# Fewer, larger zero fills and a mask on the smaller operand in a decode step with cache gradients

## The chip, the cores and the metric

One core of a Trainium2 chip. The metric is the device time of one execution in microseconds (us); a difference below 2% counts as "the same".

## The reference

One token passes through a layer norm, attention over the last 4096 of 32768 cached positions (16 heads on 8 cache heads of 256), and a gated feed-forward block; then the gradients for all inputs are formed. Only this matters here:

```python
W = min(4096, max(256, Sk // 4))                      # 4096 of Sk = 32768
k = jnp.repeat(k_cache[:, :, Sk - W:, :], rep, axis=1)
v = jnp.repeat(v_cache[:, :, Sk - W:, :], rep, axis=1)
...
_out, _vjp = jax.vjp(_f, A_x, A_k_cache, A_v_cache, A_wq, A_wo, B_w_gate, B_w_up, B_w_down)
return (_out0, *_grads)                                # shortened; two of the gradients: 8 x 32768 x 256 bf16 each
```

Seven eighths of the two cache gradients are zeros, and the kernel has to write them: 280.6 MB written against 53.7 MB read.

## The kernel before

GpSimd's queue carries the zero fills, one region of 2 MB (128 partitions x 16 KB) a transfer, from a block of zeros in SBUF. SyncE's queue carries the cache loads, the outputs and a few late fills. Fills 0 to 41 use the whole block of zeros. Then the upper half of the block is lent to weights, and 13 fills go out "in halves" from the lower half. When the weights are used, VectorE clears the upper half again and the other fills follow.

```python
ZW = 8192                       # 16 KB of zeros in each partition
HALF0, HALF1 = 42, 55
...
def send_fills(n0, n1, halves=False):
    for reg in fills[n0:n1]:
        if halves:
            ZQ.dma_start(out=reg.rearrange("p (k f) -> p k f", k=2),
                         in_=zeros[:, 0:ZW // 2].unsqueeze(1).to_broadcast([128, 2, ZW // 2]))
        else:
            ZQ.dma_start(out=reg, in_=zeros)          # ZQ = nc.gpsimd

send_fills(0, HALF0)
send_fills(HALF0, HALF1, True)
...                                                   # first pass over K and V, then the feed-forward blocks
            if n == 1:
                nc.vector.memset(ar(ZW // 2, ZW // 2), 0.0)      # the "clearing"
                send_fills(HALF1, len(fills) - 1)
...                                                   # second pass, per cache head:
            nc.vector.tensor_copy(out=rT[:], in_=r_ps[:])
            ...
            RB_ = Rbig[it % 2]
            nc.vector.tensor_tensor(out=RB_, in0=R_sb[:].unsqueeze(1).to_broadcast([128, 8, 512]),
                                    in1=tl_f[:].unsqueeze(2).to_broadcast([128, 8, 512]), op=ALU.mult)
            ...
                        nc.tensor.matmul(d_ps[:, qi]..., lhsT=rT[32 * q:32 * (q + 1), :],
                                         rhs=RB_[32 * q:32 * (q + 1), l, :], start=True, stop=True)
```

## Time and profile before

| | before |
|---|---|
| time, median of 6 runs | 797.02 us (796.6 to 797.59) |
| bytes moved | 334.77 MB, mean 421 GB/s |
| last computing instruction ends | 730.7 us |
| VectorE busy | 436.6 us |
| issues of GpSimd's queue | 106 |

The prediction below shows the lines and reads them: the 16 DMA engines are busy from end to end, and the last 63 us are transfers alone. In the profile a "packet" of a DMA queue is one row moved (16 KB in the fills and the cache loads) or one semaphore write of 4 bytes that reports a finished transfer.

### The profile page before, as it was taken

Reading aid. Unit: us, or ns where it says so; the run is one execution under the profiler, and the core shown is the slowest. Engines: PE = TensorE matmul, PEld = TensorE weight load, DVE = VectorE, ACT = ScalarE, POOL = GpSimd, SP = SyncE. Lnnn points to the kernel's source line nnn. Section 1 sums busy time; section 2 is a strip of 40 time slices with the busy share of each in tenths; the row PEclk is TensorE's granted clock in tenths of the full one; section 3 lists DMA queues with packets and bytes.
Section 4 is the critical chain, followed back from the end, with each engine's and each line's share of the span. In section 5 each row is a group of like instructions: output and inputs, shape, how many; then the busy total and the mean of one; then the engine's idle time right before and its main releaser. Section 6 shows DMA issues by size and latency. Waiting matters only on the chain.

```text
span 795.1 us, 7301 instructions
## 1 busy us (share of the span) xinstructions
PE 471.2 (59%) x2903; PEld 221.2 (28%) x2926; DVE 436.6 (55%) x629; ACT 196.0 (25%) x309; POOL 63.0 (8%) x115
## 2 busy tenths in 40 slices
PE   0459999999999999251409477673450553722000
PEld 0334434344344433121208334330220210300000
DVE  2116584765846782263690679598653874964000
ACT  0142314134132201010102126362320441534000
POOL 4000000010101111100210001000000000010000
PEclk9989999999999999555558779695555555865555
DMA  9999999999999999999999999999999999999997
GB/s 348 431 427 433 431 427 430 431 429 427 433 420 425 432 416 407 423 420 425 432 432 422 424 430 428 429 424 427 424 427 423 425 424 422 426 421 414 432 432 312
DMA packets 29688, 334.77 MB, mean 421 GB/s; under 512 B 3150, under 2 KB 6230, under 8 KB 8150
## 3 DMA queue, kind: packets, MB, share of 16 engines
q0 software_dynamic: 16832, 216.01, 64.2%
q1 hardware_dynamic: 11382, 116.68, 35.0%
q10 hardware_dynamic: 1440, 1.61, 0.6%
q8 instruction: 23, 0.38, 0.2%
q14 instruction: 11, 0.09, 0.0%
HBM read 53.69 MB, written 280.59 MB: 420 GB/s over the span
## 4 chain that ended last, share of the span: by engine, by line
PE 35%; DMA 34%; DVE 15%; ACT 4%; issue 2%; another core or an unknown queue 0%; SPq 0%; DVEq 0%; ACTq 0%
DMA out_dram<-arena 21%; PE M_ps L317 12%; PE ok_ps L320 7%; PE rows_ps L256 5%; DMA dh_bc<-in_grad_out_dram 4%; DMA arena<-in_A_k_cache_dram 4%; PE tr_ps L253 4%; DMA arena<-in_B_w_down_dram 3%; ACT arena L270 2%; DVE arena L459 2%; PE dqb_ps L502 2%; DMA arena<-in_B_w_gate_dram 2%; DVE arena L635 2%; DVE arena L428 2%; DVE arena L650 1%
## 5 line engine op out<-in xcount | busy, mean ns | idle before, releaser
L312 DVE TENSOR_TENSOR arena<-arena,p_f 128x2048 bf16<-128x2048 bf16 x64 | 145.4, 2286 | 61.3 <-PE M_ps L317 61.2
L317 PE MATMUL M_ps<-arena 128*128 128x512 bf16 x489 | 125.3, 381 | 1.9 <-issue 1.0
L643 PE MATMUL d_ps<-arena,rT 32*128 32x512 bf16 x256 | 46.1, 506 | 115.4 <-DVE arena L651 67.6
L253 PE MATMUL tr_ps<-ident_bf,arena 128*128 128x128 bf16 x1024 | 90.3, 239 | 19.7 <-ACT arena L611 11.4
L256 PE MATMUL rows_ps<-arena,vpad 128*16 128x512 bf16 x256 | 87.4, 436 | 21.0 <-DVE arena L613 15.2
L133 POOL DMA_DIRECT2D out_dram<-arena x89 | 47.4, 535 | 529.9 <-DMA out_dram<-arena 495.9
L253 PEld LDWEIGHTS <-arena 128*128 128x128 bf16 x1024 | 67.6, 107 | 71.4 <-issue 62.2
L270 ACT COPY arena<-tr_ps 128x1024 bf16<-128x1024 bf16 x64 | 61.8, 1016 | 64.5 <-PE tr_ps L253 64.5
L647 ACT CAST arena<-d_ps 128x512 bf16<-128x512 f32 x64 | 37.6, 588 | 125.0 <-PE d_ps L643 124.9
L320 PE MATMUL ok_ps<-arena 128*16 128x512 bf16 x256 | 63.8, 381 | 0.9 <-DVE arena L297 0.9
L317 PEld LDWEIGHTS <-arena 128*128 128x128 bf16 x512 | 43.3, 99 | 59.0 <-issue 23.2
L611 ACT COPY arena<-tr_ps 128x1024 bf16<-128x1024 bf16 x32 | 32.6, 1020 | 95.0 <-PE tr_ps L253 37.1
L651 DVE CAST arena<-d_ps 128x512 bf16<-128x512 f32 x64 | 43.6, 681 | 13.3 <-DMA out_dram<-arena 13.3
L650 DVE CAST arena<-d_ps 128x512 bf16<-128x512 f32 x64 | 43.9, 685 | 12.6 <-PE d_ps L643 12.0
L643 PEld LDWEIGHTS <-rT 32*128 32x128 bf16 x256 | 11.5, 95 | 141.0 <-issue 92.5
L648 ACT CAST arena<-d_ps 128x512 bf16<-128x512 f32 x64 | 38.1, 595 | 14.1 <-DMA out_dram<-arena 14.1
L635 DVE TENSOR_TENSOR arena<-R_sb,tl_f 128x4096 bf16<-128x4096 bf16 x8 | 35.4, 4419 | 0.7 <-ACT R_sb L633 0.7
L256 PEld LDWEIGHTS <-vpad 128*16 128x16 bf16 x256 | 19.0, 91 | 57.6 <-issue 49.5
L320 PEld LDWEIGHTS <-arena 128*16 128x16 bf16 x256 | 19.1, 89 | 41.5 <-issue 20.3
L514 DVE CUSTOM_DVE_ANT_0 arena<-arena 128x4096 bf16<-128x4096 bf16 x3 | 13.1, 4423 | 24.1 <-ACT arena L507 24.1
L285 ACT ACTIVATE e_f<-cols_ps,nbias 128x32 f32<-128x32 f32 x16 | 4.5, 285 | 86.9 <-DVE nbias L281 86.9
L258 DVE COPY arena<-rows_ps 16x512 f32<-16x512 f32 x16 | 10.8, 676 | 26.4 <-PE rows_ps L256 26.3
(199 smaller groups left out, 390.9 us busy)
## 6 DMA issues: line engine op xcount, KB each, us to landing
out_dram<-arena POOLq DMA_DIRECT2D x102, 2048.0 KB, 52.6
out_dram<-arena SPq DMA_DIRECT2D x18, 2048.0 KB, 32.9
arena<-in_A_v_cache_dram SPq DMA_DIRECT2D x10, 2048.0 KB, 50.2
arena<-in_A_k_cache_dram SPq DMA_DIRECT2D x8, 2048.0 KB, 29.3
out_dram<-arena SPq DMA_DIRECT2D x4, 4096.0 KB, 43.8
arena<-in_A_wq_dram SPq DMA_DIRECT2D x2, 3072.0 KB, 20.8
arena<-in_A_wo_dram SPq DMA_DIRECT2D x2, 1792.0 KB, 14.2
out_dram<-arena SPq DMA_DIRECT2D x2, 1792.0 KB, 15.3
```

The costliest lines, as they stand in the source:

```text
L133: ZQ.dma_start(out=reg, in_=zeros)
L253: nc.tensor.transpose(tr_ps[:, dh, i, :], X_sb[:, 4 * q + i, dh * 128:(dh + 1) * 128], ident_bf[:])
L256: nc.tensor.matmul(rows_ps[:], lhsT=pad[:, dh, 16 * q:16 * q + 16], rhs=XT[:, dh].rearrange("p t k -> p (t k)"), start=(q == 0 and dh == 0 ...
L270: sT_ps = dots(kv_at(K_off[g]), KT_slot, vpad[g % 2], rows1, ps_c, "cols", lambda q, XT, ps: nc.scalar.copy(out=XT, in_=ps))
L312: nc.vector.tensor_tensor(out=pK, in0=K_sb[:, 4 * c:4 * c + 4, :].unsqueeze(2).to_broadcast([128, 4, 2, Dh]), in1=p_f[:, c::8, :].unsqueez ...
L317: nc.tensor.matmul(M_ps[:, vh, :], lhsT=V_sb[:, t, vh * 128:(vh + 1) * 128], rhs=pK[:, i, :, :].rearrange("p h d -> p (h d)"), start=(t == ...
L320: nc.tensor.matmul(ok_ps[:].rearrange("p k d -> p (k d)"), lhsT=ppad[g % 2][:, 8 * (t % 4) + t // 4, :], rhs=both(g, t), start=(g == 0 and ...
L635: nc.vector.tensor_tensor(out=RB_, in0=R_sb[:].unsqueeze(1).to_broadcast([128, 8, 512]), in1=tl_f[:].unsqueeze(2).to_broadcast([128, 8, 51 ...
L643: nc.tensor.matmul(d_ps[:, qi].rearrange("p w d -> p (w d)"), lhsT=rT[32 * q:32 * (q + 1), :], rhs=RB_[32 * q:32 * (q + 1), l, :], start=T ...
L648: nc.scalar.copy(out=stK[:, t:t + 2, :], in_=d_ps[:, :, 1, :])
L650: nc.vector.tensor_copy(out=stV[:, t:t + 2, :], in_=d_ps[:, :, 0, :])
L651: nc.vector.tensor_copy(out=stK[:, t:t + 2, :], in_=d_ps[:, :, 1, :])
```

## The change

The intent: fewer and larger transfers on GpSimd's queue, and less VectorE work in the second pass. The mask (which of eight rows l a partition belongs to) is multiplied into the transposed probabilities (128 x 1024) instead of the other operand (128 x 4096); the products are the same.

```diff
+GROUP = 4
     def send_fills(n0, n1, halves=False):
-        for reg in fills[n0:n1]:
+        while n0 < n1:
+            o, g, i = fills[n0]
+            n = 1
+            while n < GROUP and n0 + n < n1 and fills[n0 + n][:2] == (o, g):
+                n += 1
+            reg = zero_rows(o, g, i, i + n, ZW)
             if halves:
                 ... (as before, one transfer a region)
             else:
-                ZQ.dma_start(out=reg, in_=zeros)
+                ZQ.dma_start(out=reg.rearrange("n p f -> p n f"), in_=zeros.unsqueeze(1).to_broadcast([128, n, ZW]))
+            n0 += n
...
-            rT = work2.tile([128, 128], bf16, tag="rT")
-            nc.vector.tensor_copy(out=rT[:], in_=r_ps[:])
+            rTm = rT_slot[it % 2]
+            nc.vector.tensor_tensor(out=rTm, in0=r_ps[:].unsqueeze(1).to_broadcast([128, 8, 128]),
+                                    in1=tl_f[:].unsqueeze(2).to_broadcast([128, 8, 128]), op=ALU.mult)
...
-            RB_ = Rbig[it % 2]
-            nc.vector.tensor_tensor(out=RB_, in0=R_sb..., in1=tl_f..., op=ALU.mult)
-                        nc.tensor.matmul(..., lhsT=rT[32 * q:32 * (q + 1), :], rhs=RB_[32 * q:32 * (q + 1), l, :],
+                        nc.tensor.matmul(..., lhsT=rTm[32 * q:32 * (q + 1), l, :], rhs=R_sb[32 * q:32 * (q + 1), :],
```

More of the change, by code (lines that the diff above doesn't have):

```diff
@@ L87 @@
     rows2 = ar(RB + 47 * KB, 2 * KB)[0:16].bitcast(f32)
-    Rbig = [ar(RB + 8 * KB * i, 8 * KB).rearrange("p (l n) -> p l n", l=8) for i in range(2)]
+    rT_slot = [ar(RB + 2 * KB * i, 2 * KB).rearrange("p (l n) -> p l n", l=8) for i in range(2)]
+    R_slot = [ar(RB + (4 + i) * KB, KB) for i in range(2)]
     dK_off = [RB + 16 * KB, A_off[2]]
@@ L124 @@
                 continue
-            reg = zero_rows(o, g, 0, 5 if g == G - 1 else NZ, ZW)
-            fills += [reg[i] for i in range(reg.shape[0])]
+            fills += [(o, g, i) for i in range(5 if g == G - 1 else NZ)]
     def send_fills(n0, n1, halves=False):
-        for reg in fills[n0:n1]:
+        while n0 < n1:
[4 more added lines that the diff above has]
+            reg = zero_rows(o, g, i, i + n, ZW)
             if halves:
-                ZQ.dma_start(out=reg.rearrange("p (k f) -> p k f", k=2), in_=zeros[:, 0:ZW // 2].unsqueeze(1).to_broadcast([128, 2, ZW // 2]))
-            else:
-                ZQ.dma_start(out=reg, in_=zeros)
+                for r in range(n):
+                    ZQ.dma_start(out=reg[r].rearrange("p (k f) -> p k f", k=2), in_=zeros[:, 0:ZW // 2].unsqueeze(1).to_broadcast([128, 2, ZW // 2]))
+            elif n == 1:
+                ZQ.dma_start(out=reg[0], in_=zeros)
+            else:
+                ZQ.dma_start(out=reg.rearrange("n p f -> p n f"), in_=zeros.unsqueeze(1).to_broadcast([128, n, ZW]))
+            n0 += n
     send_fills(0, HALF0)
@@ L631 @@
                     nc.tensor.matmul(R_ps[:, w, dh, :], lhsT=Zr[:, 2 * w + dh].rearrange("p k i -> p (k i)"), rhs=ident_bf[:], start=True, stop=True)
-            R_sb = work2.tile([128, 512], bf16, tag="R", bufs=1)
-            nc.scalar.copy(out=R_sb[:], in_=R_ps[:].rearrange("p w e n -> p (w e n)"))
-            RB_ = Rbig[it % 2]
-            nc.vector.tensor_tensor(out=RB_, in0=R_sb[:].unsqueeze(1).to_broadcast([128, 8, 512]),
-                                    in1=tl_f[:].unsqueeze(2).to_broadcast([128, 8, 512]), op=ALU.mult)
+            R_sb = R_slot[it % 2]
+            nc.scalar.copy(out=R_sb, in_=R_ps[:].rearrange("p w e n -> p (w e n)"))
             stV, stK = V_sb, kv_at(dK_off[it % 2])
@@ L642 @@
                         q = 2 * qp + qi
-                        nc.tensor.matmul(d_ps[:, qi].rearrange("p w d -> p (w d)"), lhsT=rT[32 * q:32 * (q + 1), :], rhs=RB_[32 * q:32 * (q + 1), l, :],
+                        nc.tensor.matmul(d_ps[:, qi].rearrange("p w d -> p (w d)"), lhsT=rTm[32 * q:32 * (q + 1), l, :], rhs=R_sb[32 * q:32 * (q + 1), :],
                                          start=True, stop=True)
@@ L658 @@
                 nc.vector.memset(ar(ZW, ZW), 0.0)
-        flat = fills[-1].rearrange("p f -> (p f)")
+        o, g, i = fills[-1]
+        flat = zero_rows(o, g, i, i + 1, ZW)[0].rearrange("p f -> (p f)")
         base = 0
```

## The prediction

> **What bounds the kernel now.** I looked first at the page's 40 slices and its DMA queue rows, because the kernel writes two cache gradients that are mostly zeros and so has to move a great many bytes whatever it computes.
>
> ```profile
> DMA  9999999999999999999999999999999999999997
> GB/s 348 431 427 433 431 427 430 431 429 427 433 420 425 432 416 407 423 420 425 432 432 422 424 430 428 429 424 427 424 427 423 425 424 422 426 421 414 432 432 312
> DMA packets 29688, 334.77 MB, mean 421 GB/s; under 512 B 3150, under 2 KB 6230, under 8 KB 8150
> q0 software_dynamic: 16832, 216.01, 64.2%
> q1 hardware_dynamic: 11382, 116.68, 35.0%
> ```
>
> No slice but the last is under nine tenths. q0 is GpSimd's queue (the zero fills), q1 is SyncE's. Their shares of the 16 engines' time, 64.2% and 35.0%, with 0.6% and 0.2% for two small queues, add up to 100% of the span: there is no unused DMA time in the body of this kernel. The second view is the table by stretches, which shows where the little idle time sits (columns: stretch, its length, busy time of the five engine rows, TensorE clock, DMA share, GB/s).
>
> ```profile
> 0.00:20.00 20.00, 0.37 (x1) 0.09 (x1) 4.55 (x18) 1.28 (x1) 9.46 (x18) 1.00 0.92 351
> 20.00:300.00 280.00, 256.95 (x1546) 110.02 (x1570) 163.87 (x163) 75.91 (x112) 21.56 (x39) 0.98 1.01 428
> 700.00:732.00 32.00, 6.25 (x41) 1.38 (x41) 17.55 (x22) 11.32 (x21) 2.39 (x4) 0.51 1.01 418
> 732.00:745.00 13.00, 0.00 (x0) 0.00 (x0) 0.00 (x0) 0.00 (x0) 0.00 (x0) 0.50 1.02 423
> 745.00:760.00 15.00, 0.00 (x0) 0.00 (x0) 0.00 (x0) 0.00 (x0) 0.00 (x0) 0.50 1.00 430
> 780.00:785.00 5.00, 0.00 (x0) 0.00 (x0) 0.00 (x0) 0.00 (x0) 0.00 (x0) 0.50 0.96 413
> 785.00:790.00 5.00, 0.00 (x0) 0.00 (x0) 0.00 (x0) 0.00 (x0) 0.00 (x0) 0.50 0.80 344
> 790.00:795.00 5.00, 0.00 (x0) 0.00 (x0) 0.00 (x0) 0.00 (x0) 0.00 (x0) 0.50 0.15 62
> ```
>
> All compute is over before 732; the last 63 us are transfers alone. So the computation has some 60 us of slack against the end, and only bytes, bytes per second and the two ragged ends decide. At the 428 GB/s of 20 to 300 us, 334.77 MB take 782.2 us. The first 20 us lose (428-351)/428 x 20 = 3.6 us, the last 15 us lose 5 x (15+84+366)/428 = 5.4 us; together 791.2, and the 3.9 us up to the span of 795.1 come from stretches at 418 to 423 GB/s. The most that perfect ends could give is 9 us, 1.1%.
>
> Third, the waits, because they look as if the fills were the problem:
>
> ```profile
> POOL out_dram L133 <- DMA out_dram<-arena: 495.9, 75, 9.7
> POOL out_dram L131 <- DMA out_dram<-arena: 77.0, 13, 9.7
> ```
>
> GpSimd idles 573 us for its own earlier fills. In the built program each fill waits for the fill eight places ahead of it, so eight are in flight. The page gives 52.6 us from issue to landing, and 8 x 2 MB in that time is the queue at work: this wait is flow control, not starvation. The timeline of GpSimd shows the cost of a fill with nothing beside it:
>
> ```profile
> 387.45 0.53 POOL L133 DMA_DIRECT2D out_dram<-arena  x1 [4.47 <-DMA out_dram<-arena]
> 392.33 0.53 POOL L133 DMA_DIRECT2D out_dram<-arena  x1 [4.34 <-DMA out_dram<-arena]
> 397.28 0.53 POOL L133 DMA_DIRECT2D out_dram<-arena  x1 [4.42 <-DMA out_dram<-arena]
> ...
> 416.93 0.53 POOL L133 DMA_DIRECT2D out_dram<-arena  x1 [4.38 <-DMA out_dram<-arena]
> ```
>
> Six intervals from 387.45 to 416.93 make 4.913 us each for 2.097 MB: 427 GB/s.
>
> **What the Trainium skill says.** "DMA: Bandwidth & Descriptors", section "Issuing engines are not separate DMA queues": transfers from all issuers run on the same 16 DMA engines and interleave. The shares that add to 100% agree. The same page, section "Bandwidth" (measured table), has 341 GB/s for 1 MB and 425 GB/s for 16 MB, which would promise much for larger transfers; but those are single transfers. With eight queued, this trace already has 427 GB/s at 2 MB, and the trace decides. For VectorE, "VectorE: DVE Perf Modes", section "Side-by-side", gives one element a cycle at 0.96 GHz plus some 150 ns in the slow mode. The two rows below agree: (4419-2286)/(4096-2048) = 1.04 ns an element, with 153 ns fixed.
>
> ```profile
> L312 DVE TENSOR_TENSOR arena<-arena,p_f 128x2048 bf16<-128x2048 bf16 x64 | 145.4, 2286 | 61.3 <-PE M_ps L317 61.2
> L635 DVE TENSOR_TENSOR arena<-R_sb,tl_f 128x4096 bf16<-128x4096 bf16 x8 | 35.4, 4419 | 0.7 <-ACT R_sb L633 0.7
> L626 DVE COPY rT<-r_ps 128x128 bf16<-128x128 bf16 x8 | 1.7, 214 | 0.0
> ```
>
> **The change, part by part.** First, the fills. The 102 whole-region fills (89 plain, 13 in halves) become 6 of 8 MB and 6 of 6 MB, the 13 halves as before, one of 2 MB, then 7 of 8 MB and 6 of 6 MB: 39. With the four uneven pieces at the end GpSimd issues 43 instead of 106. Bytes, rows (16 KB) and their order in the queue by regions stay. What a transfer costs on the engines beyond its rows I take from the trace's packets: a plain 16 KB row takes 611 ns, so 128 rows on 16 engines are 4.888 us of the 4.913, and 25 ns are left. 63 transfers fewer by 25 ns is 1.6 us. That lies on the path, because the engines are the bound.
>
> The halves are still sent with eight in flight, and the last of the 13 still waits for the fifth. So the upper half of the zeros is free, and GpSimd blocks for its clearing (33.9 us at L433), as before. The weights that overwrite that half wait for fill 42; in a first-in first-out queue it lands when it did.
>
> Second, the mask. Eight multiplies of 4419 ns and eight copies of 214 ns go; eight multiplies of 1024 elements from PSUM come, estimated at 153 + 1024 x 1.04 = 1.22 us. VectorE saves 8 x (4.42+0.21-1.22) = 27 us. TensorE keeps its 256 products of the same shape. From the transposed probabilities to the first product the path gets 3.4 us shorter in each of eight groups, at most 27 us. But the chain of that pass is mostly outputs landing, for example:
>
> ```profile
> 604.83 24.19 DMA out_dram<-arena
> ...
> 639.92 23.77 DMA out_dram<-arena
> ...
> 673.39 42.61 DMA out_dram<-arena
> ```
>
> Outputs sent earlier take engine time from fills, which then go later; the sum is the same. With 60 us of transfers behind the last instruction, I put the gain of this part at the end at zero.
>
> Sum: 797.19 - 1.6 - 0 = 795.6 us.
>
> **The rivals.** (a) Larger fills reach a better rate. For it: the kernel's own 4 MB transfers (32 KB rows) run at up to 438 GB/s when alone at the end. If q0's 216 MB went at 438 instead of 427, that would be 216 x (1/427 - 1/438) x 1000 = 12.7 us, some 784. Against it: the rows stay 16 KB, and I believe the row, not the transfer, makes that difference. (b) The new order of rows hurts. An engine now writes the same partition's row in 3 or 4 places 2 MB apart before the next partition. The Trainium skill's DMA page, section "Latency and other measured facts", tells of HBM tiles with a power-of-two pitch between partitions at half rate or less (164 GB/s at 2 MiB). Here the pitch between partitions, which run together on different engines, stays 16 KB, and 2 MB lies between rows of one engine that follow each other. No run yet shows this pattern. If 150 MB went 10% slower, 35 us would be added: 830. (c) Eight in flight now means up to 56 MB rather than 16: GpSimd's queue could push aside SyncE's. Against it: q0 was never empty, so its share was already what the arbitration gives; and the compute chain has 60 us of slack. Made worse by 20 us, it would still be hidden. (d) The ragged end changes: the uneven four pieces at the end were made to even out the engines, and the second pass now ends earlier, so which queue ends last may change. This moves the 5.4 us lost at the end by perhaps 3 us either way, 793 to 799.
>
> **Range and chances.** Rival (d) and run-to-run spread (796.6 to 797.59 before) set the width around 795.6; half of rival (a) stretches it downwards: 791.5 to 799. Faster by over 2% needs less than 781.2, which is under the time of all bytes at 428 GB/s: 3%. Slower by over 2% needs rival (b): 4%. The rest, 93%, is within 2%.
>
> **What would show it.** Right: DMA digits all nine again, q0's bytes at 216 MB with the mean rate at 421 to 424 GB/s, GpSimd's issues 43, its wait for fills gone or shrunken without effect, the mask multiply at about 1.2 us x8 and VectorE some 27 us less busy, the last compute instruction earlier than 730 and the transfers-only tail longer by as much. Wrong: a 16 KB row of q0 at other than 611 ns (a or b), a DMA digit under nine in the body (c), or a last 15 us that loses much more or less than 5.4 us (d).

## The result, and the profile after

| | before | after |
|---|---|---|
| time, median of 6 runs | 797.02 us (796.6 to 797.59) | 796.80 us (795.71 to 798.43) |
| ratio | | 0.9996 (95%: 0.9983 to 1.0009) |
| VectorE busy | 436.6 us | 410.4 us |
| last computing instruction ends | 730.7 us | 744.1 us |
| issues of GpSimd's queue | 106 | 43 |

A ratio here is the mean time of one kernel's fast runs over the mean of the other's in the same rounds, so it is not quite the ratio of the medians that stand beside it. The two kernels take the same time. The profile that was taken is of the slowest of the six runs (798.43 us; its span of 796.7 leaves out what lies outside the program).

The page of the changed kernel, slices, rates and the two big queues (packets, MB, share of the engines):

```profile
DMA  9999999999999999999899999999999999999997
GB/s 349 429 431 429 429 431 430 429 430 431 429 429 430 424 425 423 416 421 422 349 421 406 429 428 428 430 431 428 426 425 432 424 429 427 427 422 410 428 443 327
q0 software_dynamic: 15824, 216.01, 64.0%
q1 hardware_dynamic: 11382, 116.68, 34.9%
```

The bytes are the same, q0 has 1008 packets fewer (63 transfers x 16 engines, the semaphore writes), and there is one digit 8, in the twentieth slice, with 349 GB/s where before it was 432. The table by stretches zooms in; its last two columns are the DMA share and GB/s. First the kernel before:

```profile
380.00:385.00 5.00, 2.85 (x20) 2.06 (x19) 2.92 (x8) 1.77 (x3) 0.94 (x2) 0.50 1.04 444
480.00:700.00 220.00, 115.92 (x768) 51.09 (x766) 157.76 (x206) 86.68 (x141) 13.28 (x25) 0.67 1.01 425
```

Then the changed kernel:

```profile
380.00:385.00 5.00, 0.82 (x3) 0.33 (x4) 4.55 (x12) 0.00 (x0) 1.15 (x2) 0.50 0.35 144
385.00:390.00 5.00, 3.35 (x22) 2.20 (x21) 3.65 (x11) 1.01 (x1) 4.71 (x7) 0.50 0.99 378
480.00:700.00 220.00, 107.55 (x717) 46.80 (x714) 130.67 (x185) 80.05 (x129) 1.53 (x2) 0.67 1.01 428
```

Between 380 and 385 us the DMA engines stood still for two thirds of the time. Against 428 GB/s the two short stretches lose 5 x (284+50)/428 = 3.9 us. The long stretch from 480 to 700 us is a little faster than before: 220 x 3/428 = 1.5 us won. (The rates are printed in whole GB/s, so these are estimates good to about half a microsecond.) GpSimd's timeline says what happened at 380 us. Before:

```profile
342.62 0.66 POOL L131 DMA_DIRECT2D out_dram<-arena  x1 [5.52 <-DMA out_dram<-arena]
377.23 3.17 POOL L133 DMA_DIRECT2D out_dram<-arena  x6 [33.95 <-DVE arena L433]
```

After:

```profile
340.11 0.67 POOL L138 DMA_DIRECT2D out_dram<-arena  x1 [5.53 <-DMA out_dram<-arena]
383.85 0.55 POOL L140 DMA_DIRECT2D out_dram<-arena  x1 [43.07 <-DVE arena L443]
384.39 5.32 POOL L142 DMA_DIRECT2D out_dram<-arena  x7
```

In each pair the first line is the last fill in halves, the second the first fill after the clearing. In both kernels eight fills are in flight when GpSimd begins to wait for the clearing (L433, now L443). Before, it waited 34 us, and six of the eight had landed. Now it waits 43 us, and the queue was empty. The fills are 2.5 us earlier and the clearing 6.6 us later.

Why was the clearing later? It follows the first pass and the feed-forward blocks, and those follow SyncE's loads. From 40 to 140 us both queues always had work. The DMA view of that stretch (packets, MB, share), before:

```profile
q1 hardware_dynamic: 1472, 21.50, 50.3%
q0 software_dynamic: 1473, 21.41, 50.2%
```

After:

```profile
q0 software_dynamic: 1419, 22.46, 52.6%
q1 hardware_dynamic: 1411, 20.50, 47.9%
```

SyncE's q1 fell from 215 to 205 GB/s. What stays equal between the two queues, in both kernels, is the number of packets. So my theory, put to the test below: here the engines give each queue the same number of turns, and the semaphore write at the end of a transfer takes a turn like a row of 16 KB. A 2 MB transfer has 8 rows and one semaphore write on each engine (8 rows in 9 turns, 0.889). Fills of 8 and 6 MB have 32 rows in 33 turns and 24 in 25 (together 56 in 58, 0.966). SyncE's loads stayed at 0.889, so they should get 0.889/(0.889+0.966) of 430 GB/s = 206; measured 205. Loads later, the first pass later (the weights of the first feed-forward block are issued at 305.2 instead of 299.1 us), the clearing later, and the fill queue dry.

The second pass shows the new mask at its price; the row is operation, shapes, count, busy time, mean ns, idle before:

```profile
L636 DVE TENSOR_TENSOR arena<-r_ps,tl_f 128x1024 bf16<-128x1024 bf16 x8 | 9.7, 1214 | 0.8 <-PE r_ps L634 0.8
```

### The profile page after: what moved, and what is told of

It is laid out like the page before. It is cut to its first block, busy times and chain, and to the rows that moved or that the text cites. A ratio compares the mean times of both kernels' runs of the same rounds, so it can differ in the third digit from the quotient of the medians.

```text
span 796.7 us, 7253 instructions
## 1 busy us (share of the span) xinstructions
PE 470.7 (59%) x2926; PEld 218.9 (27%) x2926; DVE 410.4 (52%) x621; ACT 196.0 (25%) x309; POOL 35.4 (4%) x52
## 4 chain that ended last, share of the span: by engine, by line
another core or an unknown queue 36%; DMA 29%; DVE 14%; PE 9%; issue 2%; POOL 1%; ACT 1%; DVEq 0%; ACTq 0%; SPq 0%; POOLq 0%
DMA out_dram<-arena 29%; DVE arena L469 2%; DVE arena L658 2%; DVE arena L554 2%; PE rows_ps L266 2%; PE dqb_ps L512 2%; DVE arena L659 2%; PE d_ps L651 2%; PE tr_ps L263 1%; DVE arena L524 1%; DVE arena L438 1%; POOL out_dram L138 1%; PE dqb_ps L515 1%; DVE arena L623 1%
## 5 line engine op out<-in xcount | busy, mean ns | idle before, releaser
L327 PE MATMUL M_ps<-arena 128*128 128x512 bf16 x512 | 129.6, 382 | 0.2 <-ACT arena L333 0.2
L651 PE MATMUL d_ps<-arena 32*128 32x512 bf16 x256 | 44.8, 507 | 104.8 <-DVE arena L659 90.3
L651 PEld LDWEIGHTS <-arena 32*128 32x128 bf16 x256 | 10.6, 95 | 129.9 <-issue 80.0
L142 POOL DMA_DIRECT2D out_dram<-arena x25 | 19.3, 775 | 230.3 <-DMA out_dram<-arena 230.2
L549 DVE TENSOR_SCALAR arena<-arena,xT 128x1792 bf16<-128x1792 bf16 (+1 forms) x9 | 7.7, 881 | 35.5 <-DMA out_dram<-arena 35.5
```

Of the source, the lines that this page charges most:

```text
L327: nc.tensor.matmul(M_ps[:, vh, :], lhsT=V_sb[:, t, vh * 128:(vh + 1) * 128], rhs=pK[:, i, :, :].rearrange("p h d -> p (h d)"), start=(t == ...
L651: nc.tensor.matmul(d_ps[:, qi].rearrange("p w d -> p (w d)"), lhsT=rTm[32 * q:32 * (q + 1), l, :], rhs=R_sb[32 * q:32 * (q + 1), :], start ...
```

## The experiments

Each was run beside the kernel before on the same chip; the medians of before are 797.1 to 797.6 us.

### The larger fills alone

```diff
 (kernel before)
+GROUP = 4, and send_fills() of the change; the mask stays on the 128 x 4096 operand
```

> The larger fills alone, on the kernel before. My theory: the DMA engines are the bound; 63 transfers fewer give back 63 x 25 ns = 1.6 us, and a lower share of SyncE's queue (some 204 GB/s instead of 215 while both queues are full) makes the first pass late by some 6 us, so that the clearing of the zeros ends after the fill queue has run dry, which costs some 3 to 4 us. So 797 to 800 us, and the profile has a stretch near 380 us with a DMA share well under 0.9. Rival: the stretch in the profile of the changed kernel came from the new mask or was a chance of that one run; then no such stretch and 795.5 us.

Measured: 796.89 us, ratio 0.9993 (0.9980 to 1.0006). The dry stretch is there (a digit 8 and 347 GB/s in the twentieth slice), GpSimd waits 43.25 us for the clearing, and q1 has 205.1 GB/s from 40 to 140 us. So the stretch belongs to the fills, not to the mask and not to chance. The time itself lies a little under the range that I expected: loss and gain of the fills nearly cancel.

### The new mask alone

```diff
 (changed kernel)
-GROUP = 4
+GROUP = 1
```

> The new mask alone, fills of 2 MB. My theory: VectorE saves 27 us in the second pass, but the engines of the DMA are the bound, so 797.0 us, within 1 us of the kernel before; no stretch with a low DMA share near 380 us; GpSimd waits 34 us for the clearing as before. Rival (the chain of the second pass sets the end): up to 27 us less, 770 us.

Measured: 797.30 us, ratio 0.9994 (0.9982 to 1.0007); VectorE 410.4 us busy; wait for the clearing 34.5 us; no dry stretch; last computing instruction at 727.1 us. The mask is worth 26 us of VectorE, 4 us at the end of the second pass, and nothing that this interval of about 1 us can show at the end of the kernel.

### Three more fills in halves

```diff
 (changed kernel)
-HALF0, HALF1 = 42, 55
+HALF0, HALF1 = 42, 58
```

> The changed kernel with 16 fills in halves instead of 13, so that 6 MB more are in the queue while the zeros are being cleared (3 x 4.9 = 15 us of work). My theory: the dry stretch near 380 us goes, DMA share 1.0 there, and the time falls by the 3 to 4 us lost there, to some 793 to 794 us. Rival (the loss there is caught up elsewhere, for instance the queues only shift and the end is set by another thing): unchanged at 796.8 us.

Measured: 793.83 us (793.2 to 796.17), ratio 0.9956 (0.9943 to 0.9969). The same table of stretches:

```profile
380.00:385.00 5.00, 2.03 (x5) 0.57 (x6) 4.78 (x13) 0.00 (x0) 2.77 (x4) 0.50 1.02 431
480.00:700.00 220.00, 104.65 (x721) 46.85 (x718) 130.00 (x186) 79.78 (x129) 0.80 (x2) 0.67 1.01 428
```

The gap is filled, the gain of the long stretch stays, and the median falls by 3.0 us, of the estimated 3.9 that the gap had cost. This is the test of where the expected gain went. (The kernel before with 16 fills in halves was not run; its queue has no gap to fill.)

### Large fills only after the clearing

```diff
 (changed kernel)
-    def send_fills(n0, n1, halves=False):
+    def send_fills(n0, n1, halves=False, group=1):
-            while n < GROUP and ...
+            while n < group and ...
-                send_fills(HALF1, len(fills) - 1)
+                send_fills(HALF1, len(fills) - 1, group=GROUP)
```

> Large fills only after the clearing (47 fills in 14 transfers); the 55 before it go as in the kernel before. My theory: SyncE's share in the first pass is back to 215 GB/s, the first pass is as early as before, GpSimd waits 34 us for the clearing, no dry stretch, and 33 transfers fewer save 33 x 25 ns = 0.8 us: 796.0 us. Rival (the large fills of the second pass are what costs): 798 us or more with a DMA share under 1.0 after 400 us.

Measured: 793.79 us (793.4 to 795.41), ratio 0.9956 (0.9942 to 0.9969). The first pass is as early as before (q1 at 215 GB/s, wait for the clearing 33.6 us, no gap), as expected. But the gain is 3.8 us, not 0.8: my 25 ns for a transfer were far too little for this part of the kernel. The stretch from 480 to 700 us runs at 428 GB/s here too, 1.5 us of the gain. In the two profiled runs the spans differ by 2.8 us (795.1 and 792.3), and 0.8 us of that is only the ragged end (see rival d below). The last computing instruction ends at 738.6 us, against 727.1 with the new mask alone: large fills in the second pass make that pass later by themselves. From 480 to 700 us q1 moved 34.1 MB here and 36.1 MB there.

### Fewer fills in halves on the kernel before

```diff
 (kernel before)
-HALF0, HALF1 = 42, 55
+HALF0, HALF1 = 42, 52
```

> The kernel before with 10 fills in halves instead of 13: the fill queue runs dry some 15 us before the clearing of the zeros ends. My theory (idle engine time there is never given back): 804 to 808 us and a DMA share well under 0.9 between 360 and 385 us; GpSimd's wait for the clearing some 50 us. Rival (the lost time is caught up later): 797.5 us.

Measured: 808.38 us, ratio 1.0138 (1.0124 to 1.0153); GpSimd waited 53 us.

```profile
365.00:370.00 5.00, 3.25 (x37) 2.92 (x37) 0.52 (x2) 0.00 (x0) 0.00 (x0) 0.50 0.60 253
370.00:375.00 5.00, 0.00 (x0) 0.00 (x0) 4.58 (x10) 0.00 (x0) 0.00 (x0) 0.50 0.02 8
375.00:380.00 5.00, 2.02 (x5) 0.57 (x6) 4.90 (x13) 0.19 (x1) 3.13 (x6) 0.50 0.49 197
```

These three stretches lose 5 x (0.40+0.98+0.51) = 9.5 us of engine time, and the kernel became 11 us longer. Idle engine time in the middle was not caught up. It also shows how near the kernel before stood to this edge.

### Fills of 1 MB

```diff
 (kernel before)
-                ZQ.dma_start(out=reg, in_=zeros)
+                for k in range(2):
+                    ZQ.dma_start(out=reg[64 * k:64 * (k + 1)], in_=zeros[k::2])
```

> The opposite of the change, on the kernel before: each plain 2 MB fill in two of 1 MB (every second partition, rows still 16 KB), 89 transfers more. My theory of the shares: the DMA engines take one row or one semaphore write of each queue in turn, so a queue's share goes with rows per turn. A 1 MB fill is 4 rows and 1 semaphore write per engine (0.80), a load of SyncE 8 and 1 (0.889): SyncE gets 0.889/1.689 of 430 = 226 GB/s between 40 and 140 us (before 215, changed kernel 205). The time rises by 89 x 25 to 64 ns = 2.2 to 5.7 us: 799.5 to 803 us. Rival (the share moves with the megabytes in flight, not with the turns): the amount in flight halves too, so this run alone does not tell it apart; kv_split does. Rival (the number of transfers costs nothing): 797.5 us.

Measured: 1152.84 us. As a test of time this run failed. The waits show where the time went: compute, loads and fills waited for each other in places where they had not.

```profile
POOL out_dram L134 <- DVE d_hh L404: 282.8, 1, 282.8
SPq L357 <- DMA out_dram<-arena: 231.6, 2, 213.5
```

I take it that a source of every second partition is tracked as touching much more than it does; that was not tested. Before those waits the run is good for the shares. From 50 to 90 us both queues had work:

```profile
q1 hardware_dynamic: 633, 9.06, 52.9%
q0 software_dynamic: 628, 8.19, 47.9%
```

q1 has 9.06 MB in 40 us, 226.5 GB/s, where the theory of turns said 226; and again the packets are equal. (The stretch that I had named, 40 to 140 us, can't be used: the loads are over by 110 us.) The rival that transfers cost nothing is left untested by this run.

### SyncE's loads in two

```diff
 (kernel before)
-        LD.dma_start(out=kv_at(off), in_=cache[0, g, Sk - W:, :].rearrange("(p t) d -> p t d", t=T))
+        for k in range(2):
+            LD.dma_start(out=kv_at(off)[k::2], in_=cache[0, g, Sk - W:, :].rearrange("(p t) d -> p t d", t=T)[k::2])
```

> The kernel before with SyncE's cache loads of 2 MB each in two of 1 MB (every second partition); the fills and their number in flight are untouched. Theory of the turns: SyncE's rows per turn fall from 0.889 to 0.80, its share from 215 to 0.80/1.689 of 430 = 204 GB/s between 40 and 140 us, as in the changed kernel; the first pass is then some 6 us late, GpSimd waits 43 us for the clearing, a dry stretch near 380 us, 800 to 801 us. Rival (the depth of the fill queue sets the share): SyncE stays at 215 GB/s, no dry stretch, 797.5 us.

Measured: 837.84 us, again with waits that the kernel before did not have (GpSimd waited 90 us for the clearing), so its time says nothing. The shares from 40 to 80 us, where both queues had work, do:

```profile
q0 software_dynamic: 613, 8.98, 53.1%
q1 hardware_dynamic: 619, 8.14, 47.7%
```

8.14 MB in 40 us are 203.5 GB/s; the theory of turns said 204, the rival of the depth 215. The fills were untouched here, in size and in number in flight, so the depth of the fill queue is not what moves the share. The stretches of these two runs were picked after the run, for the time in which both queues had work; that the share then makes the first pass late is read from the traces and from the runs with early and late large fills, not from this one.

### Rows next to each other

```diff
 (changed kernel)
-  out=reg.rearrange("n p f -> p n f")
+  out=reg.rearrange("n p f -> (n p) f").rearrange("(p n) f -> p n f", n=n)
```

> The changed kernel with the rows of a large fill laid out so that a partition writes its 3 or 4 rows next to each other instead of 2 MB apart. My theory: the place of the rows costs nothing; 796.8 us as the changed kernel, rows of q0 at a median of 611 ns, the dry stretch near 380 us as there. Rival (steps of 2 MB in one engine cost something): under 795 us and a lower mean duration of the rows.

Measured: 796.20 us, ratio to before 0.9990 (0.9977 to 1.0002), the dry stretch still there, the mean 16 KB row of q0 from 480 to 700 us at 616.0 ns as in the changed kernel. The steps of 2 MB cost nothing that this can see.

### Six fills left out

```diff
 (changed kernel; wrong on purpose)
-                send_fills(HALF1, len(fills) - 1)
+                send_fills(HALF1, len(fills) - 7)
```

> The changed kernel without six of its zero fills (12.6 MB not written; the result is right only if that memory already holds zeros). My theory (bytes are the bound, the last computation ends some 53 us before the end): 6 x 4.91 = 29.5 us less, 767 us. Rival (the chain of computation sets the end): unchanged at 796.8 us.

Measured: 768.38 us, 28.4 us under the changed kernel's median, with two outputs wrong as intended. 12.6 MB at 428 GB/s are 29.4 us. So bytes set the end here.

### The old mask twice

```diff
 (kernel before)
             nc.vector.tensor_tensor(out=RB_, in0=R_sb..., in1=tl_f..., op=ALU.mult)
+            nc.vector.tensor_tensor(out=RB_, in0=R_sb..., in1=tl_f..., op=ALU.mult)
```

> The kernel before with its 128 x 4096 mask multiply done twice: VectorE 8 x 4.42 = 35 us busier in the second pass. My theory (the second pass has 60 us of slack behind it): 797.2 us, unchanged within 1.5 us, with the last VectorE instruction later than the 730.7 us of before. Rival (the second pass sets the end): up to 35 us more, 832 us.

Measured: 797.66 us, ratio 1.0005 (0.9992 to 1.0018). The last VectorE instruction in its timeline:

```profile
762.97 0.68 DVE L653 CAST arena<-d_ps 128x512 bf16<-128x512 f32 x1
```

That is 33 us later than in the kernel before, and the kernel ends at the same time: VectorE's work in the second pass is off the path.

### Still larger late fills, and the old mask with late fills

```diff
 (group_late)
-GROUP = 4
+GROUP = 7
```

> As group_late, with up to 7 fills in a transfer (14 MB): the 47 fills after the clearing in 8 transfers instead of 14. If the gain of group_late comes with the number of transfers at 25 to 115 ns each, 0.2 to 0.7 us less than group_late: 793.1 to 793.6 us. If it comes from anything that 6 and 8 MB transfers already give in full, 793.8 us. The descriptors may be too many for the queue; then the issue itself takes longer, with no effect on the end.

Measured: 794.00 us (793.76 to 794.31), ratio 0.9959 (0.9947 to 0.9971). Six transfers fewer show no further gain. This does not decide between the two readings that I had put up: 0.2 to 0.7 us was forecast for a fixed price per transfer, and the intervals are about 1 us wide to each side.

```diff
 (kernel before, with send_fills() of group_late; the old mask)
```

> As group_late, but with the mask of the kernel before. My theory (the mask adds nothing to the end): 793.8 us as group_late, within 1 us. Rival (the saved VectorE time is worth something once the fills are out of the way): 796 us or more.

Measured: 794.52 us (793.44 to 796.0), ratio 0.9966 (0.9954 to 0.9978), where group_late has 0.9956 (0.9942 to 0.9969). The intervals overlap, so no effect of the mask is shown; these two runs leave room for one of up to some 2 us.

The best versions are group_late and the one with 16 halves, both at 793.8 us: 3.8 us or 0.4% under their kernel before, and faster than the changed kernel as well. By the 2% rule that too is "the same".

## Why the prediction was right, and where it was wrong

**The bound: right.** 334.77 MB through engines with no free time; confirmed by leaving out bytes (28.4 us less) and by adding VectorE work (nothing).

**The mask: right on size and on effect.** 1.22 us was estimated for the new multiply, 1.214 us measured; 27 us of VectorE saved, 26.2 measured; worth nothing at the end that can be seen, and the run with the mask alone says so (ratio 0.9994, 0.9982 to 1.0007).

**"GpSimd blocks for its clearing (33.9 us at L433), as before": wrong.** It waited 43 us. I had checked the order of the queue and the number in flight, which did stay, and had not asked whether the clearing itself would come later. The kernel before had its queue nearly empty at the clearing, a margin that I did not work out.

**"q0 was never empty, so its share was already what the arbitration gives" (rival c): wrong in its reason.** The share did move, from 50.2% to 52.6%. The reading that fits all four pairs of packet counts is that the semaphore writes which the change removes had been taking turns. The conclusion of that rival, that the delay is hidden by 60 us of slack, holds for the end of the second pass (13 us later, no harm). It did not hold for the clearing, which is a second place where computation gates transfers, and which has hardly any slack.

**The 1.6 us for 63 transfers: too small.** The 25 ns were read in a stretch where only fills ran, and with the median row of 611 ns; with the mean row of that stretch, 611.8 ns, 19 ns are left, and the semaphore write itself takes 9 ns of each engine (packed trace). In the stretch from 480 to 700 us larger fills win more: 425 to 428 GB/s is 1.5 us there alone, and the run with large late fills gained 3.8 us. Then the dry stretch took some 3.9 us back. The two errors were of similar size and opposite sign, so that 795.6 came as close as it did to 796.8 was luck. The range did not depend on it: with the gap filled (16 fills in halves) the kernel takes 793.8 us, which lies in it too. What makes the late stretch faster stays open: the mean 16 KB row of q0 there fell from 619.1 to 616.0 ns (packed trace; the median stays 611), and the place of the rows is not the reason. One price per transfer for the whole kernel does not fit: by the packet counts some 19 transfers fewer finished from 480 to 700 us, and some 7 fewer from 40 to 140 us, where the rate stayed at 430 GB/s.

**"The last compute instruction earlier than 730": wrong.** It came 13 us later, at 744 us. The mask alone makes it 727, the fills alone 743, and large fills after the clearing alone, with the new mask, 738.6: the large fills delay the second pass more than the mask speeds it up, and most of that delay arises in the second pass itself.

**"DMA digits all nine": wrong by one digit.** A digit under nine in the body was the sign that the prediction had named for rival (c), and it came. The mean rate was 420 GB/s where 421 to 424 was forecast. The layout of rows (rival b) did no harm, and larger transfers did not reach 438 GB/s (rival a).

**The ragged end (rival d): as large as the gain that was looked for.** Against 428 GB/s the last 15 us lost 5.4 us before and 4.7 us after (295 GB/s over them). Over eleven profiled runs (all but the two with transfers from every second partition and the one with fills left out) this loss goes from 3.5 us (rows next to each other) to 7.0 us (the old mask twice), so differences of 1 or 2 us between single profiled runs can come from it alone. What sets it was not tested.

## What to carry to other kernels

Where the DMA engines are full from end to end, look for every place at which a computation gates the next transfers, and count how many microseconds of queued work are left there; here a change that moved 10 GB/s from one queue to the other made the clearing 6.6 us later, and that was more than the margin. In this kernel the size of the filler transfers also set how the two queues shared the engines, so make them large only where nobody waits for the other queue. A smaller VectorE operand was good housekeeping but no time, with 60 us of transfers behind the last instruction.

## What the Trainium skill lacked or had wrong

- "DMA: Bandwidth & Descriptors", section "Queues, rings and completion order", has the engines take turns between queues a packet at a time, a packet being "≈9-17 descriptors typical". What a turn holds, and whether a semaphore write is a turn of its own, is not said precisely enough to predict a share. Here the two queues moved nearly equal numbers of rows and semaphore writes together: 1473 and 1472 before, 1419 and 1411 after, 628 and 633 with fills of 1 MB, 613 and 619 with loads of 1 MB. A semaphore write of 4 bytes counted as much as a row of 16 KB, and 8 rows to 1 write against 56 to 2 moved the loads from 215 to 205 GB/s.
- The same page, section "Bandwidth" (measured table): the table has no row for several transfers in flight or for two queues at once. With eight in flight, 2 MB fills ran at 427 GB/s, and 6 to 8 MB brought 425 to 428 GB/s where two queues shared the engines.
- No page says what a transfer from every second partition does to the waits that are set when the kernel is recorded. The two runs that used such transfers took 356 us (1152.8 against 797.2) and 41 us (837.8 against 797.2) longer; that this is the cause was not tested.
